# Loading q and k onto both row halves instead of copying between them, in an attention, expert and FFN kernel on one core

## The chip, the cores and the metric

The kernel runs on one core of a Trainium2 chip. A core has five engines with an instruction queue each: PE (TensorE, the matrix engine), DVE (VectorE), ACT (ScalarE), POOL (GpSimd) and SP (SyncE), which here only issues DMAs. The metric is the device time of one execution in microseconds (us), the median of several runs.

## What is computed

The reference chains three parts in float32, for batch B = 4 and 448 positions:

```python
# 1. causal attention, 12 heads of 64
scores = scale * q @ k^T ; scores = where(triu, -1e9, scores)
attn = exp(scores - max) ; attn = attn / (attn.sum + 1e-9)
x = (attn @ v)                       # -> (4, 448, 768)
# 2. four experts of width 64, each a causal attention on x; two of four chosen per position
q, k, v = x @ wq[e], x @ wk[e], x @ wv[e]
ye = softmax_causal(scale * q @ k^T) @ v @ wo[e]
out += gate_weight[e] * ye           # weights: softmax over the two largest of x @ w_gate
# 3. FFN with a convolution over positions
h = relu(out @ w_in)                 # 768 -> 1024
gate = sigmoid(conv3(h, conv_w))
result = (h * gate) @ w_out          # 1024 -> 768
```

## The kernel before

**Number format.** Where plain float32 would be slow, a value x is split into a high part (the copy rounded to the type fp32r) and a low part (x minus the high part), and a product is done as matmuls on the parts. For the scores of a head, which contract over 64 numbers only, the parts are stacked on the 128 rows: one half of the rows holds one part of q, the other half the other, and two matmuls per block (`for k in (2, 1)`, L580) run on all 128 rows.

**Heads and pairs.** Heads are handled in pairs (a "job"). There are 24 attention pairs A (6 per batch, `order` at L428 to L431) and 8 expert pairs M. Pair tensors in HBM have head 0 on rows 0 to 63 and head 1 on rows 64 to 127, q and k side by side.

**Preparing a pair** (`prep`, L515). An attention pair is loaded once as `nat`, 128 rows x 2 x 448 (L522). `hi` (L528) copies q and k to the high parts in `sk[0]`, `lo` (L532) subtracts for the low parts, in one instruction on POOL (L324). The parts now lie on the head's own half of the rows. `stack` (L457) moves them with five DMAs from SBUF to SBUF: three for head 1 (`go_b`, L467), then two for head 0 (`go_a`, L475). The first pair of all goes another way (`prep_twice`, L481): each head is loaded onto both halves by two DMAs, one on SP's queue and one on ACT's (L494), split at L497 and subtracted at L501 and L505, with no copies. Expert pairs come from a projection (`proj_qk`, L866) and use `stack` too.

**A head** (`head`, L559). Its 448 queries are four blocks of 112. For block i = 3, 2, 1, 0: two score matmuls (L581) of width 112 (i + 1) into a PSUM bank; DVE adds the causal mask, takes the row maximum and copies the scores out (`rowmax`, L594), which frees the bank; ACT takes the exponential with row sums (`soft`, L603). Then sums and reciprocals (L611, L614), normalisation (`norm`, L317 on POOL or L315 on ACT), transposes on PE (L634) into a bank and their copy to SBUF (`evac`, L315 or L321), and the products with v of both heads (L695, full float32, head h on output rows 64 h to 64 h + 63).

**Around it.** While the attention of batch 0 runs, `fold_all` (L756) multiplies the expert output weights into w_in: twelve pieces are loaded, converted from float64 bit by bit (`from_f64`, L372: four DVE and one ACT instruction), split and multiplied (L804). The projections of x (L880, L926) need its memory, so they start when it ends. The FFN (L1096 to L1160) starts when the projections are over and w_out is converted in the same way.

**What sets the order.** The kernel is a list of tasks with an engine (or several allowed ones, `ON`), an estimated cost, a priority, and ring buffers or PSUM banks taken and freed. `Program.run` (L129) simulates the engines with these costs when the kernel is built: whenever an engine is free it takes the ready task of lowest priority number whose buffers are free, and emits its instructions. On the chip each engine then runs its instructions in that fixed order. Priorities are 8 per job (`slot`) plus the numbers of `PR`; a task allowed on several engines carries an extra number (`PR["other"]`) on all but the first. A load counts 3200 ns to landing. A task with POOL among its engines, or marked `port`, holds a lock that keeps such tasks on DVE and POOL apart in the simulation. Where PE would be idle over 700 ns, `warm` (L1231) emits dummy matmuls on the identity (L1237) into an idle bank.

**Rings and banks.** `RINGS` gives the number of buffers (P = 3 for a head's scores, nat = 1, skA = 2 for the stacked parts of attention pairs), `BANKS` the PSUM banks per use: scores s = (0, 1), transposes t = (2, 3), products with v = (4, 5).

Of the kernel before, what the change touches and what calls it, by code (L numbers as in the profile page):

```python
# [16 lines left out]
AX = mybir.AxisListType  # L17

# [210 lines left out]
def attn_moe_ffn_kernel(  # L229
# [34 lines left out]
    BANKS = dict(s=(0, 1), t=(2, 3), v=(4, 5), m=(6, 7), h=(6, 7, 0, 2), o=(5, 3, 1))  # L264
    RINGS = dict(
        P=3, PT=4, osb=4, nat=1, skA=2, vn=3, vw=2, skM=1, vm=1, wg=2,
# [4 lines left out]
        load=(-823.5, 6881.0, -9741.0, -3861.0), prep=(-3868.5, 1311.5, -4485.0, 2630.5), wproj=-5653.5,  # L271
        fold0=2436.0, fold=6416.0, qk0=(-13000.5, -741.5, -2927.0, 9516.0), v=(1625.5, 634.5, 907.0, 9618.5),
        qk1=(9913.0, 10105.0, 5929.0, 31345.5), evac=-5114.5, conv=-6013.5,
        wo=(-7231.0, 5032.5, 7570.5, 14511.5, 8967.5, -5685.5), ffn0=564.5,
        ffn=(10002.0, -5113.5, 5693.5, -1579.0), out=(-702.0, 5485.0, -763.5, 1469.5),
        score=(8996.0, -638.0, 1743.0, -7812.5), rmax=(-1352.5, 6783.0, 22485.0, -7290.0),
        exp=(6192.0, 5875.5, 2412.5, 7853.5), norm=(4557.0, 1209.5, -5988.0, 7065.0),
        tr=(9656.0, -270.0, -15605.5, -1081.5), ev=(1749.0, 6735.5, -9228.0, 7657.5),
        pv=(-1538.5, 604.0, -2977.5, -6617.5), add=(-15863.0, 9244.5, -2422.5, -15681.0),
        slot=(-12628.0, 989.5, -130.0, -4172.5, 1485.5, 2137.0, -3585.0, -3863.5, -3413.5, -2921.5, -3458.0, -2327.0, -2434.0, -7790.5, -2832.0, 758.0, -1208.5, -1106.0, 8414.5, 976.0, 2099.0, 259.5, 4120.0, -1073.0, 3327.5, 6014.5, 6970.5, 8079.5, 6526.0, 4369.0, 3369.0, 3946.5),  # L280
        other=(8535.5, 4618.5, -2299.5, 867.0, 2856.0, 749.0, -4170.5), rows=(5476.0, 3097.0),
# [167 lines left out]
    def alloc_sk(j):  # L449
        n = f"{j.kind}{j.b}_{j.p}"  # L450
        pool = pools["head" if j.kind == "A" else "m"]
        j.sk = [
            pool.tile([P, 4 - h, S], F32R, tag=f"sk{h}", name=f"sk{h}_{n}", bufs=RINGS["sk" + j.kind])
            for h in range(2)
        ]
# [25 lines left out]
    def prep_twice(j):  # L481

        ready = {}
        for h in (1, 0):
            st = {}
            o = 1 - h

            def load(h=h, st=st):
                if h == 1:
                    alloc_sk(j)  # L490
                t = pools["a"].tile([P, TRI], F32, tag="PT", name=f"nat{h}", bufs=RINGS["PT"])
                st["nat"] = t[:, : 2 * S].rearrange("p (a n) -> p a n", a=2)
                for half in range(2):
                    (nc.scalar if half else nc.sync).dma_start(st["nat"][half * D : (half + 1) * D], qk[j.b, j.p, h * D : (h + 1) * D])  # L494

            def hi(h=h, st=st, o=o):
                nc.scalar.activation(j.sk[h][:, o : o + 3 : 2, :], st["nat"], AF.Copy)  # L497

            def lo_k(h=h, st=st, o=o):
                t = j.sk[h]  # L500
                nc.vector.tensor_tensor(t[:, o + 1, :], st["nat"][:, 1], f(t[:, o + 2, :]), ALU.subtract)  # L501

            def lo_q(h=h, st=st, o=o):
                q = j.sk[h][D:P, o, :]
                nc.vector.tensor_tensor(q, st["nat"][D:P, 0], f(q), ALU.subtract)  # L505

            pr = j.slot - 20 + o
            nb = Buf("PT")
            t = add("SP", pr, 1500, load, take=[j.skb, nb] if h == 1 else [nb], lag=3200)
            t = add("ACT", pr, act_sb(2 * S), hi, [t])  # L510
            tk = add("DVE", pr, dve(S), lo_k, [t], port=True)
            ready[h] = add("DVE", pr, dve(S), lo_q, [tk], free=[nb], port=True)
        return ready

    def prep(j):  # L515
        n = f"{j.b}_{j.p}"
        nat = Buf("nat")
        j.skb, j.vb = Buf("skA"), Buf("vn")

        def load():  # L520
            j.nat = pools["head"].tile([P, 2, S], F32, tag="nat", name=f"nat_{n}", bufs=1)
            nc.sync.dma_start(j.nat, qk[j.b, j.p])  # L522
# [5 lines left out]
        def hi(e):  # L528
            alloc_sk(j)
            copy(e, j.sk[0][:, 1:4:2, :], j.nat)  # L530

        def lo(e):  # L532
            t = j.sk[0]
            two(e, t[:, 0:3:2, :], j.nat, f(t[:, 1:4:2, :]), ALU.subtract)

        if j is order[0]:
            j.ready = prep_twice(j)
        else:
            t = add("SP", j.slot + PR["load"][j.phase], 1300, load, take=[nat], lag=3200)
            eng = either("q_hi", j.phase, of_one(2 * S))  # L540
            th = add(eng, j.slot + PR["prep"][j.phase], 0, hi, [t], take=[j.skb], free=[nat])
            eng = either("ql", j.phase, of_two(2 * S))
            tl = add(eng, j.slot + PR["prep"][j.phase], 0, lo, [th], free=[nat])
            stack(j, j.slot + PR["prep"][j.phase], [th, tl])
        j.vready = [add("SP", j.slot + PR["load"][j.phase] + 2, 700, load_v, take=[j.vb], lag=3200)]
# [3 lines left out]
    def attend(j):  # L549
# [4 lines left out]
        j.PT, j.evs = {}, []  # L554
        for h in (1, 0):
            head(j, h, moe)
        products_v(j, moe)

    def head(j, h, moe):  # L559
        n = f"{j.kind}{j.b}_{j.p}_{h}"  # L560
        prio = j.slot + 4 * (1 - h)
        st = {}
        Pb = Buf("P")
# [5 lines left out]
        def score(i):  # L569
            def go():  # L570
                if i == NQ - 1:
                    st["P"] = pools["a"].tile([P, TRI], F32, tag="P", name=f"P_{n}", bufs=RINGS["P"])[:CP]
                    st["sm"] = sums[n_head[0] % len(sums)]
                    n_head[0] += 1
                    for key in ("nm", "r"):
                        st[key] = pools["a"].tile([CP, NQ], F32, tag=key, name=f"{key}_{n}", bufs=RINGS["P"])
                w = CP * (i + 1)
                st["s", i] = sp = ps(st["sb", i])
                t = j.sk[h]
                for k in (2, 1):  # L580
                    nc.tensor.matmul(  # L581
                        sp[:CP, :w],
                        t[:, 1 - h, i * CP : (i + 1) * CP],
                        t[:, 1 - h + k, :w],
                        start=(k == 2),
                        stop=(k == 1),
                    )
# [714 lines left out]
```

## Time and profile before

| | us |
|---|---|
| median of 3 runs (lowest to highest) | 556.37 (553.23 to 557.66) |
| the profiled execution, its time | 555.16 |
| its span, first to last instruction | 553.4 |
| PE busy in the span | 517.9 |
| DVE busy, ACT busy, POOL busy | 348.1, 348.2, 226.5 |

The profile records one execution. A row of `xN` merges N instructions; "L581" is line 581 of the kernel. "PEq", "SPq" are sequencers. Matmuls are pipelined, so their durations overlap, and PE can be "busy" with dummy matmuls. What stands after an arrow is what ended an idle time.

### The profile page before, as it was taken

Reading aid. Unit: us, or ns where it says so; the run is one execution under the profiler, and the core shown is the slowest. Engines: PE = TensorE matmul, PEld = TensorE weight load, DVE = VectorE, ACT = ScalarE, POOL = GpSimd, SP = SyncE. Lnnn points to the kernel's source line nnn. Section 1 sums busy time; section 2 is a strip of 40 time slices with the busy share of each in tenths; the row PEclk is TensorE's granted clock in tenths of the full one; section 3 lists DMA queues with packets and bytes.
Section 4 is the critical chain, followed back from the end, with each engine's and each line's share of the span. In section 5 each row is a group of like instructions: output and inputs, shape, how many; then the busy total and the mean of one; then the engine's idle time right before and its main releaser. Section 6 shows DMA issues by size and latency. Waiting matters only on the chain.

```text
span 553.4 us, 10183 instructions
## 1 busy us (share of the span) xinstructions
PE 517.9 (94%) x3306; PEld 439.3 (79%) x3306; DVE 348.1 (63%) x1081; ACT 348.2 (63%) x931; POOL 226.5 (41%) x375
## 2 busy tenths in 40 slices
PE   6977979999998989999989999997999999999997
PEld 6766757878786777888768887876789999899996
DVE  3778988685475574766652856578999914955000
ACT  3869989786575675578764865559868504844111
POOL 1555566645564465575544643362543110000000
PEclk8889999999999998999999999998999999999999
DMA  8889986887648376749396134352130210010111
GB/s 251 239 213 234 232 234 162 245 207 173 157 101 184 93 168 166 174 111 221 85 199 158 25 76 124 106 132 58 38 116 34 71 51 33 18 42 26 50 51 66
DMA packets 28230, 70.91 MB, mean 128 GB/s; under 512 B 4433, under 2 KB 12241, under 8 KB 28177
## 3 DMA queue, kind: packets, MB, share of 16 engines
q1 hardware_dynamic: 28016, 69.80, 49.1%
q8 instruction: 26, 0.43, 0.3%
q10 hardware_dynamic: 160, 0.46, 0.3%
q14 instruction: 28, 0.22, 0.1%
HBM read 32.74 MB, written 5.51 MB: 69 GB/s over the span
## 4 chain that ended last, share of the span: by engine, by line
PE 61%; DMA 14%; DVE 11%; POOL 5%; ACT 4%; issue 3%; SPq 3%; POOLq 0%; ACTq 0%; DVEq 0%
PE bank L1160 18%; PE bank L880 10%; PE bank L581 10%; PE bank L634 7%; DMA sk_A<-sk_A 7%; PE bank L695 7%; DMA nat<-in_qk_dram 4%; PE bank L1096 4%; PE bank L926 4%; DVE bank L1117 3%; POOL sk_A L324 3%; SPq L467 2%; DMA woraw<-in_w_out_dram 2%; DVE g L1134 1%; DVE P_A L594 1%
## 5 line engine op out<-in xcount | busy, mean ns | idle before, releaser
L1160 PE MATMUL bank<-g,wout 128*128 128x448 f32 x576 | 119.4, 366 | 0.0
L603 ACT ACTIVATE P_A<-P_A,nm_A 112x448 f32<-112x448 f32 x192 | 99.6, 521 | 26.7 <-DVE nm_A L594 24.9
L1160 PEld LDWEIGHTS bank<-g,wout 128*128 128x128 f32 x576 | 108.1, 188 | 8.8
L317 POOL TENSOR_SCALAR P_A<-P_A,r_A 112x336 f32<-112x336 f32 (+3 forms) x169 | 83.6, 513 | 67.0 <-DVE r_A L614 43.9
L594 DVE CUSTOM_DVE_ANT_0 P_A<-bank,mask 112x448 f32<-112x448 f32 x192 | 80.8, 442 | 40.2 <-PE bank L581 33.3
L581 PE MATMUL bank<-sk_A 128*112 128x112 f32 (+3 forms) x384 | 81.9, 324 | 17.7 <-DMA sk_A<-sk_A 10.4
L581 PEld LDWEIGHTS bank<-sk_A 128*112 128x112 f32 x384 | 58.1, 182 | 31.6 <-DVE nm_A L594 10.5
L880 PE MATMUL bank<-xT,wqk 128*128 128x448 f32 x288 | 75.0, 381 | 0.1
L324 POOL TENSOR_TENSOR sk_A<-nat,sk_A 128x896 fp32r<-128x896 f32 x23 | 48.6, 2112 | 44.4 <-ACT sk_A L315 35.8
L634 PE MATMUL bank<-ident,P_A 112*112 112x112 f32 x480 | 64.8, 265 | 2.1 <-ACT PT_A L315 1.6
L634 PEld LDWEIGHTS bank<-ident,P_A 112*112 112x112 f32 x480 | 51.2, 135 | 7.2 <-POOL P_A L317 1.1
L1117 DVE SCALAR_TENSOR_TENSOR bank<-h,cw,bank 128x448 f32<-128x448 f32 x64 | 42.2, 682 | 17.0 <-ACT bank L1115 16.8
L880 PEld LDWEIGHTS bank<-xT,wqk 128*128 128x128 f32 x288 | 49.9, 191 | 3.0 <-DVE wqk L856 0.5
L695 PE MATMUL bank<-PT_A,v 112*64 112x448 f32 (+3 forms) x384 | 51.3, 408 | 0.0
L315 ACT ACTIVATE osb<-bank 128x448 f32<-128x448 f32 x18 | 9.8, 543 | 61.1 <-PE bank L1160 61.1
L1096 PE MATMUL bank<-ocs,wp 128*128 128x448 f32 x192 | 43.9, 376 | 2.8 <-DVE g L1134 2.0
L321 DVE TENSOR_SCALAR PT_A<-bank 112x448 f32<-112x448 f32 (+1 forms) x71 | 38.8, 556 | 11.4 <-PE bank L634 9.9
L695 PEld LDWEIGHTS bank<-PT_A,v 112*64 112x64 f32 x384 | 25.8, 137 | 24.6 <-issue 13.9
L926 PE MATMUL bank<-wvg,xT 128*112 128x260 f32 x288 | 45.2, 293 | 0.1
L315 ACT ACTIVATE PT_A<-bank 112x336 f32<-112x336 f32 (+1 forms) x73 | 32.8, 464 | 17.9 <-PE bank L634 13.9
L317 POOL TENSOR_SCALAR P_M<-P_M,r_M,g_w 112x448 f32<-112x448 f32 (+3 forms) x58 | 33.2, 584 | 23.0 <-DVE r_M L614 15.0
L1096 PEld LDWEIGHTS bank<-ocs,wp 128*128 128x128 f32 x192 | 36.1, 192 | 7.7 <-DVE g L1134 3.3
(103 smaller groups left out, 811.6 us busy)
## 6 DMA issues: line engine op xcount, KB each, us to landing
nat<-in_qk_dram SPq DMA_DIRECT2D x23, 448.0 KB, 5.1
sk_A<-sk_A SPq DMA_DIRECT2D x46, 224.0 KB, 4.2
sk_A<-sk_A SPq DMA_DIRECT2D x23, 336.0 KB, 3.5
wraw<-in_w_in_dram SPq DMA_DIRECT2D x12, 512.0 KB, 6.0
woraw<-in_w_out_dram SPq DMA_DIRECT2D x12, 512.0 KB, 4.0
v<-in_v_dram SPq DMA_DIRECT2D x24, 224.0 KB, 5.2
out_dram<-osb SPq DMA_DIRECT2D x24, 224.0 KB, 1.9
sk_A<-sk_A SPq DMA_DIRECT2D x46, 112.0 KB, 4.3
```

The source lines that it names most:

```text
L317: nc.gpsimd.tensor_scalar(dst, src, scale, 1.0 if scale2 is None else scale2, ALU.mult, ALU.mult)
L324: (nc.gpsimd if e == "POOL" else nc.vector).tensor_tensor(dst, a, b, op)
L581: nc.tensor.matmul(sp[:CP, :w], t[:, 1 - h, i * CP : (i + 1) * CP], t[:, 1 - h + k, :w], start=(k == 2), stop=(k == 1),)
L594: nc.vector.tensor_tensor_reduce(rows(i), st["s", i][:CP, :w], mask[:, S - w :], -SCALE, 3.0e38, ALU.add, ALU.min, st["nm"][:, i : i + 1],)
L603: nc.scalar.activation(rows(i), rows(i), AF.Exp, bias=st["nm"][:, i : i + 1], scale=-1.0, accum_out=st["sm"][:, i, 0:1],)
L634: nc.tensor.transpose(pt[:CP, o : o + CP], rows(i)[:, kt * CP : (kt + 1) * CP], ident[:CP, :CP])
L695: nc.tensor.matmul(st["ov"][h * D : (h + 1) * D, kt * CP : S], j.v[:, kt, h, :], j.PT[h][:, col_base[kt] : col_base[kt] + S - kt * CP], st ...
L880: nc.tensor.matmul(st["ps"][:, :S], proj["wqk"][:, a, cc, w, p * P : (p + 1) * P], xT[b, cc][:, b2, :], start=(cc == 0 and (a, b2) == PASS ...
L926: nc.tensor.matmul(st[i][:CP, :VW], xT[b, cc][:, a, i * CP : (i + 1) * CP], proj["wvg"][:, b2, cc, :], start=(cc == 0 and (a, b2) == PASSE ...
L1096: nc.tensor.matmul(st["ps", c][:, :S], wp[:, a, ec, c * P : (c + 1) * P], st["oc", ec][:, b2], start=(ec == 0 and (a, b2) == PASSES[0]), s ...
L1117: nc.vector.scalar_tensor_tensor(y, h, w, y, ALU.mult, ALU.add)
L1160: nc.tensor.matmul(st["ps"][:, :S], ffn["wout", n][:, a, c], gs[c][:, b2], start=(c == 0 and (a, b2) == PASSES[0]), stop=(c == NFC - 1 and ...
```

## The change

1. The first two attention pairs of batch 0 (`j.plain`) are loaded once and used as they are: scores in plain float32, q and k of a head on its own 64 rows, one matmul per block and head, both heads' matmuls one after the other in one task (`pair_scores`). Pair 0 is loaded in two halves, on ACT's and SP's queues; pair 1 in one DMA.
2. All other attention pairs are loaded like the first pair before: each head onto both halves of the rows by two DMAs of 64 rows (both on SP), then one split and two subtractions per head. The split may go to the engines of `q_hi` as before (ACT alone after batch 0), the subtractions to POOL or DVE (before: POOL). `stack` stays for expert pairs. `sk[0]` of attention pairs has three rows instead of four.
3. Blocks 1 and 0 of a head's scores share one bank, written by one task; row maxima, exponentials and the rest stay as they are. Score banks become (0, 1, 4), transpose banks (2, 3, 5).
4. P = 4 instead of 3 (with a fourth `sums` tile), nat = 2 instead of 1.
5. All numbers of `PR` are new, and the planner's cost term PVX is 10 instead of 55.

```diff
-    BANKS = dict(s=(0, 1), t=(2, 3), v=(4, 5), m=(6, 7), h=(6, 7, 0, 2), o=(5, 3, 1))
+    BANKS = dict(s=(0, 1, 4), t=(2, 3, 5), v=(4, 5), m=(6, 7), h=(6, 7, 0, 2), o=(5, 3, 1))
     RINGS = dict(
-        P=3, PT=4, osb=4, nat=1, skA=2, vn=3, vw=2, skM=1, vm=1, wg=2,
+        P=4, PT=4, osb=4, nat=2, skA=2, vn=3, vw=2, skM=1, vm=1, wg=2,
...
-        ql=('P', 'P', 'P', 'P'), norm=('PA', 'P', 'P', 'PD'), vm=('AD', 'A', 'A', 'A'), q_hi=('DAP', 'A', 'A', 'A'),
+        ql=('PD', 'PD', 'PD', 'P'), norm=('PA', 'P', 'P', 'PD'), vm=('AD', 'A', 'A', 'A'), q_hi=('DAP', 'A', 'A', 'A'),
...
-    PVX = 55
+    PVX = 10
...
+        j.plain = j.kind == "A" and j.b == 0 and j.p < 2
...
+            def go():
                 if h == 1:
                     alloc_sk(j)
...
+                st["nat"] = pools["head"].tile([P, 2, S], F32, tag="nat", name=f"nat_{n}_{h}", bufs=RINGS["nat"])
                 for half in range(2):
...
+                    nc.sync.dma_start(st["nat"][half * D : (half + 1) * D], qk[j.b, j.p, h * D : (h + 1) * D])
...
+        def hi(h, st):
+            return lambda e: copy(e, j.sk[h][:, 0:3:2, :], st["nat"])
+
+        def lo_k(h, st):
+            return lambda e: two(e, j.sk[h][:, 1, :], st["nat"][:, 1], f(j.sk[h][:, 2, :]), ALU.subtract)
+
+        def lo_q(h, st):
+            return lambda e: two(e, j.sk[h][D:P, 0, :], st["nat"][D:P, 0], f(j.sk[h][D:P, 0, :]), ALU.subtract)
+
+        def load_plain():
+            alloc_sk(j)
+            j.qk = f(j.sk[0][:, 0:2, :])
+            if j is order[0]:
+                for h in range(2):
+                    (nc.sync if h else nc.scalar).dma_start(j.qk[h * D : (h + 1) * D], qk[j.b, j.p, h * D : (h + 1) * D])
+            else:
+                nc.sync.dma_start(j.qk, qk[j.b, j.p])
...
+        if j.plain:
+            t = add("SP", j.slot + PR["load"][j.phase], 1300, load_plain, take=[j.skb], lag=3200)
+            j.ready = [t, t]
         else:
...
+            for h in (1, 0):
+                st, nat = {}, Buf("nat")
+                pr = j.slot + PR["prep"][j.phase] + 1 - h
+                take = [j.skb, nat] if h else [nat]
+                t = tl = add("SP", j.slot + PR["load"][j.phase] + 1 - h, 1400, load(h, st), [tl], take=take, lag=3200)
+                t = add(either("q_hi", j.phase, of_one(2 * S)), pr, 0, hi(h, st), [t])
+                eng = either("ql", j.phase, of_two(S))
+                tk = add(eng, pr, 0, lo_k(h, st), [t], free=[nat])
+                j.ready[h] = add(eng, pr, 0, lo_q(h, st), [tk], free=[nat])
...
+    def pair_scores(j):
...
+                w = CP * (i + 1)
+                for h in (1, 0):
...
+                    r = slice(h * D, (h + 1) * D)
+                    nc.tensor.matmul(
+                        sp[:CP, :w], j.qk[r, 0, i * CP : (i + 1) * CP], j.qk[r, 1, :w], start=True, stop=True
+                    )
...
+                for m, o in ((i, 0),) if i > 1 else ((1, 0), (0, 2 * CP)):
+                    w = CP * (m + 1)
+                    st["s", m] = sp = ps(st["sb", i])[:, o : o + w]
```

## Rows read from the trace of the kernel before

**Rows 1.** Windows, five stages: busy us (instructions) per engine, granted clock, DMA share, GB/s.

```profile
0.00:20.00 20.00, 15.42 (x78) 13.96 (x79) 8.85 (x35) 10.80 (x26) 5.65 (x17) 0.83 0.84 249
20.00:97.00 77.00, 66.25 (x488) 53.28 (x486) 66.32 (x200) 65.79 (x182) 44.41 (x47) 0.98 0.86 217
97.00:365.00 268.00, 257.42 (x1832) 212.03 (x1831) 165.53 (x650) 176.78 (x535) 145.29 (x252) 0.99 0.59 143
365.00:420.00 55.00, 49.30 (x283) 41.53 (x283) 49.24 (x99) 42.30 (x91) 22.49 (x38) 0.97 0.33 91
420.00:553.40 133.40, 129.48 (x635) 118.45 (x633) 58.13 (x100) 52.58 (x100) 8.64 (x24) 1.00 0.12 44
sum 553.40, PE 517.86 PEld 439.26 DVE 348.07 ACT 348.24 POOL 226.49; mean PE 103.57 PEld 87.85 DVE 69.61 ACT 69.65 POOL 45.30
```

**Rows 2.** The same windows, the dummy matmuls of L1237 alone: PE, weight loads.

```profile
0.00:20.00 20.00, 10.17 (x56) 9.88 (x56) 0.83 0.84 249
20.00:97.00 77.00, 3.03 (x20) 2.55 (x20) 0.98 0.86 217
97.00:365.00 268.00, 0.62 (x4) 0.53 (x4) 0.99 0.59 143
365.00:420.00 55.00, 9.77 (x74) 9.02 (x74) 0.97 0.33 91
```

**Rows 3.** PE's waits, 0 to 97 us: total us, times, longest.

```profile
PE bank L581 <- DMA sk_A<-sk_A: 6.6, 5, 2.5
PE bank L581 <- DVE nm_A L594: 3.3, 7, 1.1
```

**Rows 4.** PE's waits, 97 to 365 us.

```profile
PE bank L581 <- DMA sk_A<-sk_A: 3.8, 4, 2.1
PE bank L581 <- DVE nm_M L594: 3.3, 2, 2.7
```

**Rows 5.** Time line of the start: start us, us, engine, line, operation, idle before.

```profile
6.80 1.28 ACT L497 ACT_TABLE_LOAD   x1 [6.80 <-DMA nat<-in_qk_dram]
...
10.49 1.36 PE L581 MATMUL bank<-sk_A 128*112 128x448 f32 x4 [2.23 <-DVE sk_A L505]
...
23.34 0.95 PE L581 MATMUL bank<-sk_A 128*112 128x448 f32 x4
24.22 2.11 PE L695 MATMUL bank<-PT_A,v 112*64 112x448 f32 x16
...
36.74 0.63 PE L581 MATMUL bank<-sk_A 128*112 128x448 f32 x2 [2.46 <-DMA sk_A<-sk_A]
```

**Rows 6.** The page's DMA issues: count, KB each, median us to landing.

```profile
nat<-in_qk_dram SPq DMA_DIRECT2D x23, 448.0 KB, 5.1
sk_A<-sk_A SPq DMA_DIRECT2D x46, 224.0 KB, 4.2
sk_A<-sk_A SPq DMA_DIRECT2D x23, 336.0 KB, 3.5
...
sk_A<-sk_A SPq DMA_DIRECT2D x46, 112.0 KB, 4.3
```

**Rows 7.** Groups by line and form: busy us, mean ns, idle before.

```profile
L315 ACT ACTIVATE sk_A<-nat 128x896 fp32r<-128x896 f32 x21 | 19.9, 948 | 22.3 <-DMA nat<-in_qk_dram 14.5 <-PE bank L581 4.2 <-PE bank L634 2.5
...
L1078 POOL TENSOR_TENSOR ocs<-oc,ocs 128x448 fp32r<-128x448 f32 x8 | 9.1, 1147 | 0.2
...
L501 DVE TENSOR_TENSOR sk_A<-nat,sk_A 128x448 fp32r<-128x448 f32 x2 | 1.3, 626 | 8.1 <-ACT sk_A L497 8.1
```

**Rows 8.** ACT's waits, 97 to 365 us.

```profile
ACT sk_A L315 <- DMA nat<-in_qk_dram: 13.2, 7, 3.7
```

**Rows 9.** The instructions of L856 on DVE: ns min/median/max, first and last start.

```profile
L856 DVE TENSOR_TENSOR wqk<-praw,wqk x6: 674/680/1216, 95.6 to 112.9; 128x512 fp32r<-128x512 f32 x6
```

**Rows 10.** Time line of POOL and DVE around 110 us.

```profile
108.94 2.11 POOL L324 TENSOR_TENSOR sk_A<-nat,sk_A 128x896 fp32r<-128x896 f32 x1 [0.53 <-ACT sk_A L315]
...
110.38 1.22 DVE L856 TENSOR_TENSOR wqk<-praw,wqk 128x512 fp32r<-128x512 f32 x1
```

More of the change, by code (lines that the diff above doesn't have):

```diff
@@ L451, in alloc_sk @@
         pool = pools["head" if j.kind == "A" else "m"]
+        j.o = (0, 0) if j.kind == "A" else (1, 0)
         j.sk = [
-            pool.tile([P, 4 - h, S], F32R, tag=f"sk{h}", name=f"sk{h}_{n}", bufs=RINGS["sk" + j.kind])
+            pool.tile([P, 3 if j.kind == "A" else 4 - h, S], F32R, tag=f"sk{h}", name=f"sk{h}_{n}", bufs=RINGS["sk" + j.kind])
             for h in range(2)
@@ L479, in stack, with prep, load @@
         j.ready = [ta, tb]
[L481 to L488, printed above, removed]
+    def prep(j):
+        n = f"{j.b}_{j.p}"
+        j.skb, j.vb = Buf("skA"), Buf("vn")
+        def load(h, st):
+            def go():
                 if h == 1:
                     alloc_sk(j)
-                t = pools["a"].tile([P, TRI], F32, tag="PT", name=f"nat{h}", bufs=RINGS["PT"])
-                st["nat"] = t[:, : 2 * S].rearrange("p (a n) -> p a n", a=2)
+                st["nat"] = pools["head"].tile([P, 2, S], F32, tag="nat", name=f"nat_{n}_{h}", bufs=RINGS["nat"])
@@ L507, in prep_twice @@
[L507 to L522, printed above, removed]
+                    nc.sync.dma_start(st["nat"][half * D : (half + 1) * D], qk[j.b, j.p, h * D : (h + 1) * D])
@@ new lines, in load @@
+            return go
+        def hi(h, st):
[12 more added lines that the diff above has]
+                nc.sync.dma_start(j.qk, qk[j.b, j.p])
@@ L526, in load_v @@
             nc.sync.dma_start(j.v, v[j.b, j.p])
[L528 to L537, printed above, removed]
-        else:
[L539 to L544, printed above, removed]
+        if j.plain:
+            t = add("SP", j.slot + PR["load"][j.phase], 1300, load_plain, take=[j.skb], lag=3200)
+            j.ready = [t, t]
+        else:
+            j.ready = {}
+            tl = None
+            for h in (1, 0):
[7 more added lines that the diff above has]
+                j.ready[h] = add(eng, pr, 0, lo_q(h, st), [tk], free=[nat])
         j.vready = [add("SP", j.slot + PR["load"][j.phase] + 2, 700, load_v, take=[j.vb], lag=3200)]
@@ L554, in attend @@
         j.PT, j.evs = {}, []
+        j.st = {h: {} for h in (1, 0)}
+        if j.plain:
+            pair_scores(j)
         for h in (1, 0):
@@ L561, in head @@
         prio = j.slot + 4 * (1 - h)
-        st = {}
-        Pb = Buf("P")
+        st = j.st[h]
+        Pb = st["Pb"] if j.plain else Buf("P")
         ex, nm = {}, {}
@@ L571, in go @@
                 if i == NQ - 1:
[L572 to L587, printed above, removed]
+                    head_tiles(j, h)
+                for m, o in ((i, 0),) if i > 1 else ((1, 0), (0, 2 * CP)):
+                    w = CP * (m + 1)
+                    st["s", m] = sp = ps(st["sb", i])[:, o : o + w]
+                    t = j.sk[h]
+                    for k in (2, 1):
+                        nc.tensor.matmul(
+                            sp[:CP],
+                            t[:, j.o[h], m * CP : (m + 1) * CP],
+                            t[:, j.o[h] + k, :w],
+                            start=(k == 2),
+                            stop=(k == 1),
+                        )
             return go
@@ L651, in head @@
             w = CP * (i + 1)
-            sb = st["sb", i] = Buf("s")
-            t = add(
-                "PE", prio + PR["score"][j.phase], mm(w, 2), score(i), [j.ready[h]] + (first or late),
-                take=[sb] if first else [sb, Pb], free=[j.skb],
-            )
-            if not first:
-                first = j.taken = [t]
+            if j.plain:
+                t = j.scored[i]
+                sb = st["sb", i]
+            elif i:
+                sb = st["sb", i] = Buf("s")
+                t = add(
+                    "PE", prio + PR["score"][j.phase], mm(w, 2) + (mm(CP, 2) if i == 1 else 0), score(i), [j.ready[h]] + (first or late),
+                    take=[sb] if first else [sb, Pb], free=[j.skb],
+                )
+                if not first:
+                    first = j.taken = [t]
+                ts = t
+            else:
+                t = ts
             t = add("DVE", prio + PR["rmax"][j.phase], dve(w) + 8, rowmax(i), [t], free=[sb])
```

63 lines of the change are left out of this document (43 added, 20 removed).

## The prediction

> **What bounds the kernel now.** I read the table of stages first [rows 1]. PE is busy 517.86 of 553.40 us, so 35.54 us are idle. Part of the busy time does no work: the planner fills gaps with dummy matmuls (L1237), nearly all in three stages [rows 2]. Idle plus dummy time is the most that better feeding of PE can return in a stage:
>
> 0 to 20: 20.00 - 15.42 + 10.17 = 14.8 us. 20 to 97: 77.00 - 66.25 + 3.03 = 13.8 us. 97 to 365: 268.00 - 257.42 + 0.62 = 11.2 us. 365 to 420: 55.00 - 49.30 + 9.77 = 15.5 us. 420 to the end: 3.9 us.
>
> So there are two kinds of stage. Up to 97 us, where the attention of batch 0 runs beside the folding of the weights, no engine is full: from 20 to 97 DVE works 66.32 and ACT 65.79 of 77 us (86% and 85%), and the DMA share is 0.86. That is a pipeline that starts late and is then near several limits at once. From 97 to 365 PE is 96% busy and is the bound; only its gaps can go. From 365 on the FFN runs, which the edit touches by its new order numbers alone.
>
> Next I read who ends PE's waits [rows 3, 4]. Up to 97 us the copies between row halves end 6.6 us of them and DVE's row maxima 3.3 us. From 97 to 365 the copies of the attention pairs end 3.8 us and the row maxima 3.3 us. The time line of the start shows the lag behind these sums [rows 5]: the first pair's scores start at 10.49 us, the second's at 23.34, the third's at 36.74, the last straight after a wait for a copy.
>
> **The first two pairs in plain rows.** Pair 0 loses the load of its data onto both halves (four loads of 224 KB become two), two ACT splits and four DVE subtractions; pair 1 loses one ACT split, a POOL subtraction of 2.1 us and five copies. ACT today waits until 6.80 us for data, then comes its table load of 1.28 us, then the splits [rows 5]. In plain rows PE can start when the data lands. I take the 6.8 us of the row, though half the bytes should land sooner: 10.49 - 6.8 = 3.7 us earlier. If the table load then stands ahead of the first exponential, that gives back up to 1.3 us; ends -3.7 and -2.4, I take -3.
>
> PE itself pays in full float32: eight matmuls on 64 rows per pair instead of sixteen on 128. The trace has none on 64 rows. The nearest are the products with v, also float32 and with the same columns (448, 336, 224 and 112 for each of two heads), the two heads on different halves of the output: 16 of them in 2.11 us [rows 5]. If the two row halves overlap as these output halves do, a pair's scores cost 2.1 us; if not, twice that, 4.2. Today the four wide score matmuls of a head take 0.95 us [rows 5]; the four narrow ones have 43% of their columns, so a pair is 2 x 0.95 x 1.43 = 2.7 us. The change is between -0.6 and +1.5 us per pair; PE has 14.8 us to spare in this stage, so I cost it at nothing. Without that cover it is at most 3 us.
>
> Pair 1 no longer waits for load, split, subtraction and two rounds of copies. Its scores can follow pair 0's by about 3 us instead of 12.9. Its softmax then fills DVE and ACT time that is empty now: before 20 us DVE works 8.85 and ACT 10.80 us [rows 1].
>
> **Both halves loaded, no copies (22 pairs).** Removed per pair: one load of 448 KB and five copies, 2 x 224 + 336 + 2 x 112 = 1008 KB [rows 6]; added: four loads of 224 KB. So 1456 KB become 896. Six such pairs (numbers 2 to 7) load before 97 us: 3.4 MB less of the 21.7 MB moved there (249 GB/s for 20 us and 217 for 77), so the DMA share falls from 0.86 to about 0.7 at an equal rate. On SP seven issues per pair (with v) become five, and the waits of the copies for POOL go. What remains there is the wait of a load for its buffer, now also for the pair's tile, with v and weight loads queued behind it.
>
> The ready time of a pair shortens by two rounds of copies, 3.5 to 4.3 us to landing each [rows 6]. In return there is more to compute. ACT: two splits of 0.95 us instead of one. The subtractions: one POOL instruction of 2.11 us becomes four, of 1.15 us each on POOL (4.6 us) or 0.63 us on DVE (2.5 us) [rows 7, 10]. The planner prefers POOL and gives to DVE when DVE has nothing else; I take half each, +0.2 us on POOL and +1.25 us on DVE per pair. The ends are all on POOL (+2.5 us there per pair) and all on DVE (+2.5 us there, -2.1 on POOL). From 97 to 365 this lies beside PE: ACT works 177, DVE 166 and POOL 145 of 268 us, so 16 pairs x 0.95 = 15 us more on ACT is hidden by 91 idle us; on the path it would be 15 us. Before 97 us it is not wholly hidden: ACT gets 6 x 0.95 less the three splits saved, +2.9 us, DVE 6 x 1.25 less 2.5 saved, +5 us, against 10.7 and 11.2 idle us from 20 to 97. I count half of DVE's, 2.5 us.
>
> ACT also waits in order for loads, 13.2 us in 7 waits from 97 to 365 [rows 8], with exponentials and evacuations behind. There will be twice as many such instructions, on loads that meet 38% less traffic of q and k; I take no change.
>
> **Three banks, two blocks in one.** A head takes three score buffers instead of four, from three banks instead of two, and a fourth P buffer lets a further head start. This acts on PE's waits for row maxima, 3.3 us before 97 and 3.3 after [rows 3, 4]. It adds no instruction; the row maximum of the second last block waits for the two small matmuls of the last. Bounds 0 and 6.6 us; I take 1 us of the first, where copies would soon end the wait instead, and half of the second, 1.7.
>
> **New order numbers.** They move every engine's order. I cannot derive a sign; I take 0 within 4 us either way for the stages from 365 on (19.4 us of idle plus dummy time).
>
> **Sum.** Up to 97 us: start -3, copies ahead of PE -6.6, banks -1, DVE +2.5: -8. From 97 to 365: copies -3.8, banks -1.7, of which 2 us return as waits for the last subtraction: -3.5. The granted clock is 0.98 from 20 to 97 and 0.99 from 97 to 365 [rows 1], 0.02 x 77 + 0.01 x 268 = 4.2 us; with fewer gaps I take back 1.5. Total -13. The span goes from 553.4 to 540.4 us. The profiled execution took 555.16 us, 1.8 us around its span, so 542.2 us; it lay 1.2 us under the median of the runs (556.37), so I predict **543 us**, 13.4 us or 2.4% below.
>
> **Rivals.**
>
> *Hidden anyway, about 553 us.* From 20 to 97 us DVE and ACT are already 86% and 85% busy and get more work. If they, not the copies, set the pace of 12 to 13 us per pair, the 6.6 us only change their name. Then the 3 us of the start remain and the rest is given back as waits on subtractions: 556.4 - 3 = 553. For it: those two shares. Against: DVE's idle time in that stage is 10.7 us, and PE's waits there name copies. It includes the case that the change does not do what it says, because a subtraction queued behind normalisations on POOL is ready as late as the copy was.
>
> *Slower, about 564 us.* DVE and POOL get in each other's way. One case shows it [rows 9, 10]: the subtraction at L856 has a median of 680 ns, but the one that began at 110.38 us, while a POOL subtraction of 2.11 us was running since 108.94, took 1216 ns: 0.54 us lost. If all 88 new subtractions lose that, 47 us of stalls arise on the two engines, with row maxima behind them on DVE and normalisations on POOL. If 45% of it reaches PE the price is 21 us, 543 + 21 = 564. It decides the sign once more than 28% (13.4 us) gets through. Against it: POOL is 54% busy from 97 to 365, so many meet no POOL instruction, and DVE has 102 idle us there.
> The Trainium skill states the rule in "SBUF — State Buffer", section "SBUF: two separate sides": a DVE instruction with two SBUF inputs and a GpSimd instruction that reads SBUF exclude each other for the whole instruction. The case above agrees.
>
> *Better, about 530 us.* The start runs a full 10 us ahead, DVE and ACT fill up to 97 us, and the gaps from 97 to 365 go entirely: -15 and -11 us. For it: pairs 1 and 2 can be ready 10 us or more earlier. Against: the stages from 365 on do not shrink, and the added ACT and DVE work is real.
>
> **How the numbers follow.** Forecast 0.53, better 0.20, hidden 0.16, slower 0.11. A measurement of this kernel tells about 1% from no change, here 5.6 us. Faster by over 1%: all of "better" and all of the forecast, whose own range is 536 to 549: 0.73. Same: 0.16. Slower: 0.11. The range for 8 in 10 reaches into both neighbours: 530 to 557 us.
>
> **What would show it.** Right: first scores near 7 us, the second pair's near 10; no copies of attention data left; PE's waits for them gone with little in their place; the first projection matmul well before 97 us; the DMA share near 0.7 up to there. Wrong: PE waiting for subtractions on POOL or DVE by the 10.4 us that the copies cost (6.6 + 3.8); subtractions on DVE near 1.2 us; ACT waiting over 25 us for loads; dummy matmuls after 365 us growing past 9.8 us.

## Result and profile after

The changed kernel takes 538.69 us (535.41 to 540.93) against 556.49 us for the kernel before: ratio 0.972, 95% interval 0.968 to 0.976. (The quotient of the two medians is 0.968, at the edge of that interval; the comparisons below go by such ratios.) The forecast was 543 us, in a range of 530 to 557. The profiled execution took 538.64 us, its span 536.8.

The stages in the same windows as [rows 1] (busy us per engine, granted clock, DMA share, GB/s):

```profile
0.00:20.00 20.00, 15.74 (x85) 13.16 (x86) 8.50 (x40) 9.71 (x30) 5.44 (x15) 0.91 0.95 234
20.00:97.00 77.00, 73.79 (x578) 60.55 (x578) 71.91 (x223) 72.43 (x201) 61.90 (x78) 1.00 0.63 177
97.00:365.00 268.00, 262.15 (x1899) 219.00 (x1896) 188.02 (x677) 196.17 (x571) 156.30 (x258) 1.00 0.44 111
...
sum 536.80, PE 517.81 PEld 442.35 DVE 364.10 ACT 361.10 POOL 249.84; mean PE 103.56 PEld 88.47 DVE 72.82 ACT 72.22 POOL 49.97
```

From 20 to 97 us DVE and ACT are now busy 93% and 94% of the time (86% and 85% before) and the DMA share is 0.63 instead of 0.86. PE's idle time over the span fell from 35.5 to 19.0 us, but its busy time is the same, 517.8 us, and it holds more dummy matmuls, 34.3 us (L1280) against 23.6. So PE's useful busy time, without the dummies, fell by 10.8 us, though the work is the same but for two pairs.

To see where the end moved, I cut the windows at the first FFN matmul. Its start, before and after, from the time lines:

```profile
367.76 1.47 PE L1096 MATMUL bank<-ocs,wp 128*128 128x448 f32 x6
```

```profile
351.69 1.48 PE L1139 MATMUL bank<-ocs,wp 128*128 128x448 f32 x6
```

It comes 16.1 us earlier, and the end of the span 16.6 us. What follows takes as long as before, 185.1 us against 185.6. The two stages ahead of it, before:

```profile
0.00:97.00 97.00, 81.66 (x563) 67.25 (x563) 75.17 (x235) 76.59 (x208) 50.06 (x63) 0.95 0.86 223
97.00:367.80 270.80, 260.21 (x1853) 213.55 (x1852) 168.33 (x655) 177.90 (x537) 147.64 (x257) 0.99 0.59 143
```

and after, with the dummies of L1280 alone in the same windows below:

```profile
0.00:97.00 97.00, 89.53 (x660) 73.71 (x662) 80.41 (x263) 82.14 (x230) 67.34 (x93) 0.98 0.70 189
97.00:351.70 254.70, 251.73 (x1837) 209.77 (x1833) 178.97 (x650) 186.09 (x546) 153.67 (x255) 1.00 0.44 110
```

```profile
0.00:97.00 97.00, 19.73 (x132) 18.09 (x132) 0.98 0.70 189
97.00:351.70 254.70, 4.66 (x30) 3.90 (x30) 1.00 0.44 110
```

Up to the FFN, idle plus dummy time went from 25.9 + 13.8 = 39.7 us to 10.4 + 24.4 = 34.8 us. That is 4.9 us: 1.3 us up to 97 us (28.5 to 27.2) and 3.6 us from there to the FFN (11.2 to 7.6). The other 11.2 us are useful busy time, 328.0 against 316.9 us.

About half of that goes with the clock. At 0.95 and 0.99 the old stages lacked 0.05 x 97 + 0.01 x 271 = 7.6 us of full speed, the new ones 0.02 x 97 = 1.9, so 5.7 us; summed in windows of 2 us, with the dummies left out, it is 7.3 against 0.9 us. The old kernel's granted clock is at or near half speed (0.50, 1.2 GHz) from about 10 to 18 us and in three later spells, here with PE first; in each of them PE is busy all the time:

```profile
38.00:42.00 4.00, 4.00 (x24) 4.00 (x24) 3.15 (x14) 3.42 (x12) 3.53 (x3) 0.57 0.58 144
178.00:182.00 4.00, 4.00 (x19) 3.73 (x18) 2.40 (x12) 2.27 (x8) 2.23 (x4) 0.57 0.84 179
208.00:212.00 4.00, 4.00 (x19) 3.41 (x21) 1.80 (x9) 2.34 (x8) 1.92 (x4) 0.59 0.98 222
```

They lack 5.1 us of full speed. Each comes soon after one of PE's three longest waits of that stretch, the one that ends at 36.74 us [rows 5] and these two:

```profile
176.37 0.40 PE L581 MATMUL bank<-sk_M 128*112 128x112 f32 x2 [2.69 <-DVE nm_M L594]
...
207.92 0.94 PE L581 MATMUL bank<-sk_A 128*112 128x448 f32 x4 [2.08 <-DMA sk_A<-sk_A]
```

Two of the three are waits for copies. In the changed kernel PE never waits over 1.6 us at once between 20 us and the FFN, and up to there the clock is below 0.9 only from 14 to 20 us. Not every such wait has a spell behind it (in e9 below, one of 2.1 us for a copy has none), and no run changes the clock alone, so that the waits bring the spells is likely but not shown.

The other half goes with longer runs of the same operation. The matmuls of the two projections come in some 70 and 45 stretches before and in some 40 and 16 after, and their groups take less busy time (PE, busy us and mean ns), first before, then after; what such a run is worth by itself is not tested:

```profile
L880 PE MATMUL bank<-xT,wqk 128*128 128x448 f32 x288 | 75.0, 381 | 0.1
...
L926 PE MATMUL bank<-wvg,xT 128*112 128x260 f32 x288 | 45.2, 293 | 0.1
```

```profile
L923 PE MATMUL bank<-xT,wqk 128*128 128x448 f32 x288 | 67.2, 373 | 0.0
...
L969 PE MATMUL bank<-wvg,xT 128*112 128x260 f32 x288 | 38.2, 286 | 0.5 <-DVE sk_M L939 0.5
```

PE's waits up to 97 us, and from 97 to 365, answering [rows 3, 4]:

```profile
PE bank L574 <- DMA sk_A<-in_qk_dram: 2.2, 1, 2.2
...
PE bank L617 <- DVE sk_A L325: 0.9, 1, 0.9
PE bank L617 <- POOL sk_A L325: 0.9, 3, 0.4
...
PE bank L574 <- DVE nm_A L630: 0.3, 1, 0.3
```

```profile
PE bank L617 <- DMA sk_M<-sk_M: 2.7, 1, 2.7
...
PE bank L617 <- DVE sk_A L325: 0.3, 1, 0.3
PE bank L617 <- DVE nm_M L630: 0.2, 1, 0.2
```

The 10.4 us for copies are gone, and the subtractions that replace them (L325) cost PE 2.1 us. The waits for row maxima fell from 6.6 us to 0.5. The 2.7 us for copies of an expert pair end at 361.75 us, behind the first FFN matmul.

The start, answering [rows 5]:

```profile
9.03 1.01 PE L574 MATMUL bank<-sk_A 64*112 64x448 f32 x4 [2.15 <-DMA sk_A<-in_qk_dram]
...
15.19 2.30 PE L617 MATMUL bank<-sk_A 128*112 128x448 f32 x8 [0.44 <-POOL sk_A L325]
...
30.69 1.01 PE L574 MATMUL bank<-sk_A 64*112 64x448 f32 x4
```

Pair 0 starts 1.5 us earlier than before. The second to start is a split pair (L617, 15.19 us against 23.34 for the second pair before); the second plain pair follows only at 30.69. The new order put it there.

### The profile page after: what moved, and what is told of

The parts are those of the page before. It is cut to its first block, busy times and chain, and to the rows that moved or that the text cites. A ratio compares the mean times of both kernels' runs of the same rounds, so it can differ in the third digit from the quotient of the medians.

```text
span 536.8 us, 10287 instructions
## 1 busy us (share of the span) xinstructions
PE 517.8 (96%) x3392; PEld 442.4 (82%) x3392; DVE 364.1 (68%) x1102; ACT 361.1 (67%) x962; POOL 249.8 (47%) x404
## 4 chain that ended last, share of the span: by engine, by line
PE 70%; ACT 10%; DVE 8%; DMA 4%; POOL 4%; issue 2%; SPq 1%; DVEq 0%; ACTq 0%; POOLq 0%
PE bank L1203 20%; PE bank L738 9%; PE bank L617 9%; PE bank L670 8%; PE bank L923 8%; PE bank L969 7%; PE bank L1139 6%; ACT P_A L639 3%; PE bank L1280 2%; DMA nat<-in_qk_dram 2%; PE bank L847 2%; ACT sk_A L316 2%; POOL P_A L318 1%; DMA woraw<-in_w_out_dram 1%; POOL sk_A L325 1%
## 5 line engine op out<-in xcount | busy, mean ns | idle before, releaser
L318 POOL TENSOR_SCALAR P_A<-P_A,r_A 112x448 f32<-112x448 f32 (+3 forms) x175 | 97.5, 575 | 41.3 <-DVE r_A L650 20.2
L639 ACT ACTIVATE P_A<-P_A,nm_A 112x448 f32<-112x448 f32 (+1 forms) x192 | 99.6, 523 | 10.9 <-DVE nm_A L630 9.4
L630 DVE CUSTOM_DVE_ANT_0 P_A<-bank,mask 112x448 f32<-112x448 f32 (+1 forms) x192 | 77.8, 442 | 13.6 <-PE bank L574 9.2
L923 PE MATMUL bank<-xT,wqk 128*128 128x448 f32 x288 | 67.2, 373 | 0.0
L617 PE MATMUL bank<-sk_A 128*112 128x448 f32 (+3 forms) x352 | 64.3, 314 | 2.5 <-DVE sk_A L325 1.3
L325 POOL TENSOR_TENSOR sk_A<-nat,sk_A 64x448 fp32r<-64x448 f32 (+1 forms) x46 | 55.8, 1212 | 19.3 <-DVE sk_A L322 11.2
L617 PEld LDWEIGHTS bank<-sk_A 128*112 128x112 f32 x352 | 49.1, 178 | 9.2 <-POOL sk_A L325 1.8
L318 POOL TENSOR_SCALAR P_M<-P_M,r_M,g_w 112x336 f32<-112x336 f32 (+3 forms) x58 | 34.9, 615 | 37.8 <-DVE r_M L650 16.4
L639 ACT ACTIVATE P_M<-P_M,nm_M 112x448 f32<-112x448 f32 (+1 forms) x64 | 33.1, 519 | 12.3 <-DVE nm_M L630 12.1
L316 ACT ACTIVATE sk_A<-nat 128x896 fp32r<-128x896 f32 x39 | 36.7, 945 | 5.2 <-DMA nat<-in_qk_dram 5.0
```

The source lines that it names most:

```text
L316: nc.scalar.activation(dst, src, AF.Copy, scale=scale)
L318: nc.gpsimd.tensor_scalar(dst, src, scale, 1.0 if scale2 is None else scale2, ALU.mult, ALU.mult)
L325: (nc.gpsimd if e == "POOL" else nc.vector).tensor_tensor(dst, a, b, op)
L617: nc.tensor.matmul(sp[:CP], t[:, j.o[h], m * CP : (m + 1) * CP], t[:, j.o[h] + k, :w], start=(k == 2), stop=(k == 1),)
L630: nc.vector.tensor_tensor_reduce(rows(i), st["s", i][:CP, :w], mask[:, S - w :], -SCALE, 3.0e38, ALU.add, ALU.min, st["nm"][:, i : i + 1],)
L639: nc.scalar.activation(rows(i), rows(i), AF.Exp, bias=st["nm"][:, i : i + 1], scale=-1.0, accum_out=st["sm"][:, i, 0:1],)
```

## Experiments

All ratios are to the kernel before, timed on the same chip in the same session; two experiments are compared by their ratios. "Fitted" means that the numbers of PR were searched anew for that structure: a random search changes one to three of them at a time and keeps what shortens the planner's own estimate.

**e1: one cost term of the planner.** `PVX = 10` back to 55 in the changed kernel.

```diff
-    PVX = 10
+    PVX = 55
```

> The changed kernel (538.7 us) with the planner's cost term PVX at 55 as before instead of 10: the same instructions in a slightly other order. It measures what an order that fits a little less well costs by itself. If orders matter little: 535 to 543 us. If the new order numbers carry the gain and are finely fitted to their costs: 545 us or more.

Measured 549.41 us, ratio 0.987 (0.980 to 0.994). Nothing but the order differs (and the dummies that go with it), and by the ratios 1.5% is lost, over half of the gain. Another order of the same instructions moves the time as much as a whole part of the change.

**e2: all parts, old order.** The changed kernel with PR and PVX of before.

```diff
-    PR = dict(load=(-2419.0, 19933.0, ...
-    PVX = 10
+    PR = dict(load=(-823.5, 6881.0, ...
+    PVX = 55
```

> The changed kernel with all order numbers and PVX of before: every structural part of the change, none of the new order. Theory 'structure' (no copies and the earlier start give most of it): 541 to 548 us. Rival 'order' (the new numbers give it): 553 us or more.

Measured 558.29 us, ratio 1.007 (1.004 to 1.011): 0.7% slower than before. The parts alone, under the order written for the old kernel, bring nothing. No attention copies are left to wait for and the granted clock is 1.00 in every stage, but up to 365 us PE is idle for 14.0 us and on dummies for 34.2, together 48.2 us against 39.7 before [rows 1, 2]. The gaps are now in the plan, where the dummies fill them.

**e3: new order, no part.** The kernel before with PR and PVX of the change.

```diff
-    PR = dict(load=(-823.5, 6881.0, ...
-    PVX = 55
+    PR = dict(load=(-2419.0, 19933.0, ...
+    PVX = 10
```

> The kernel before with the new order numbers and PVX = 10, nothing else. Theory 'structure': no gain, 554 to 565 us, since PE still waits for copies. Rival 'order': 548 us or less.

Measured 599.89 us, ratio 1.079 (1.073 to 1.084), far above both ranges. PE's longest wait in total is for row maxima, which free the score banks:

```profile
PE bank L581 <- DVE nm_A L594: 12.8, 23, 3.2
```

"Order" (the new numbers give the gain by themselves) falls by e3, and "structure" as e2 states it falls by e2: order numbers belong to one structure. To compare parts, each variant needs an order of its own.

**e4: halves alone, old order.** The kernel before with the new `prep` for all pairs but the first, nat = 2 and ql on POOL or DVE.

```diff
-        P=3, PT=4, osb=4, nat=1, skA=2, vn=3, vw=2, skM=1, vm=1, wg=2,
+        P=3, PT=4, osb=4, nat=2, skA=2, vn=3, vw=2, skM=1, vm=1, wg=2,
...
-        ql=('P', 'P', 'P', 'P'), norm=...
+        ql=('PD', 'PD', 'PD', 'P'), norm=...
...
-            stack(j, j.slot + PR["prep"][j.phase], [th, tl])
+            for h in (1, 0):
...
+                j.ready[h] = add(eng, pr, 0, lo_q(h, st), [tk], free=[nat])
```

> The kernel before with one part of the change: q and k loaded onto both halves for all attention pairs (nat = 2, subtractions on POOL or DVE), no copies for them; old banks, old order numbers, no plain pairs. Theory 'copies': they are the largest part, 543 to 549 us. Rival 'hidden anyway': 553 us or more, the added splits and subtractions on ACT, DVE and POOL take back what the copies cost.

Measured 568.08 us, ratio 1.022 (1.017 to 1.027). By itself it could mean "hidden anyway"; after e2 and e3 it can as well be the order, which was written for another structure; e11 separates the two.

**e5: copies back, fitted.** The changed kernel with the preparation of before for all but the plain pairs.

```diff
-            for h in (1, 0):
-                st, nat = {}, Buf("nat")
...
+            t = add("SP", j.slot + PR["load"][j.phase], 1300, load1, take=[nat], lag=3200)
...
+            stack(j, j.slot + PR["prep"][j.phase], [th, tl])
```

> The changed kernel with the preparation of before put back for all but the two plain pairs (one load, one split, one subtraction, five copies) and everything else kept, its order numbers searched anew for this structure with the planner's own estimate, which comes out 1% shorter than for the changed kernel. Theory 'slip': copies land later than the planner counts, so the chip falls behind the plan: 548 to 558 us. Rival 'fit': only the fit of the order to the structure matters: 531 to 541 us.

Measured 549.56 us, ratio 0.995 (0.991 to 0.999), as "slip" expects, though the planner expects less time than for the changed kernel. PE's waits name the copies:

```profile
PE bank L640 <- DMA sk_A<-sk_A: 9.0, 7, 3.2
PE bank L693 <- DVE xT L786: 4.8, 1, 4.8
```

**e6: the kernel before, fitted in the same way.** Only PR (and PVX = 10) differ from the kernel before.

```diff
-        load=(-823.5, 6881.0, -9741.0, -3861.0), ...
+        load=(-985.0, 80089.0, 46435.0, -47006.5), ...
-    PVX = 55
+    PVX = 10
```

> The kernel before (all its parts, PVX = 10) with order numbers searched anew in the same way; the planner expects 1% less than for the changed kernel. Theory 'slip': 546 to 558 us, no better than before. Rival 'fit': 530 to 541 us, the changed kernel's gain without any of its parts.

Measured 561.32 us, ratio 1.016 (1.008 to 1.024). "Fit" falls: an order that the planner likes better than the changed kernel's is 4.5% slower than it on the chip when the structure is the old one. The time is also above the 558 us of "slip", and the new order is 1.6% slower than the one that this structure had: the planner's estimate does not rank orders of one structure that closely. PE waits 6.9 us for copies of attention pairs and 4.1 for those of expert pairs:

```profile
PE bank L595 <- DMA sk_A<-sk_A: 6.9, 6, 1.9
...
PE bank L595 <- DMA sk_M<-sk_M: 4.1, 3, 2.1
```

**e7: no plain pairs, fitted.**

```diff
-        j.plain = j.kind == "A" and j.b == 0 and j.p < 2
+        j.plain = False
```

> The changed kernel without plain pairs (pairs 0 and 1 split and loaded on both halves like the others), order searched anew; the planner expects 0.5% more. If plain rows give the 3 us of the start that the prediction counts: 541 to 547 us. If they give nothing: 536 to 541 us.

Measured 541.87 us, ratio 0.978 (0.972 to 0.985). The time lies in the range of "they give the 3 us", and the ratio is 0.6% (3.5 us) above the changed kernel's. But the two intervals overlap, so the plain pairs' share cannot be told from nothing.

**e8: old banks, fitted.**

```diff
-    BANKS = dict(s=(0, 1, 4), t=(2, 3, 5), v=(4, 5), m=(6, 7), h=(6, 7, 0, 2), o=(5, 3, 1))
+    BANKS = dict(s=(0, 1), t=(2, 3), v=(4, 5), m=(6, 7), h=(6, 7, 0, 2), o=(5, 3, 1))
```

> The changed kernel with the PSUM banks of before, s = (0, 1) and t = (2, 3), the last two blocks still in one bank, order searched anew; the planner expects 0.3% more. If the third bank gives the 2.7 us counted: 540 to 545 us. If it gives nothing: 536 to 540 us.

Measured 547.99 us, ratio 0.991 (0.986 to 0.996), more than either theory gave. Not by PE's waits for row maxima, 1.7 us up to 97 us in this run; the larger ones there are for subtractions on DVE and for the plain data:

```profile
PE bank L631 <- DVE sk_A L339: 4.4, 4, 2.1
PE bank L588 <- DMA sk_A<-in_qk_dram: 3.7, 2, 2.4
```

and the granted clock is 0.96 from 0 to 97 us, with a spell near half speed from 20 to 28 us around the waits for the plain data. PE's work comes later; the first FFN matmul starts at 360.2 us. Which of these the banks cause and which this order, the run does not tell.

**e9: copies back, planned with later landings, fitted.** As e5, with longer delays in the planner.

```diff
-        tb = add("SP", prio, 1900, go_b, need, lag=3300)
-        ta = add("SP", prio, 1400, go_a, need + [tb], lag=3300)
+        tb = add("SP", prio, 1900, go_b, need, lag=4800)
+        ta = add("SP", prio, 1400, go_a, need + [tb], lag=4800)
...
-            t = add("SP", j.slot + PR["load"][j.phase], 1300, load1, take=[nat], lag=3200)
+            t = add("SP", j.slot + PR["load"][j.phase], 1300, load1, take=[nat], lag=4400)
```

> As e5 (copies back in the changed kernel), but the planner now counts 1.5 us more to the landing of each round of copies and 1.2 us more for the loads, and the order is searched anew under these delays; it expects 0.2% more than for the changed kernel. Theory 'slip' (the copies cost mainly because the order was written for landings that come late): 538 to 545 us, waits of PE for copies under 4 us. Rival 'copies cost by themselves' (their time cannot be hidden by any order): 547 us or more, waits as in e5.

Measured 548.54 us, ratio 0.987 (0.982 to 0.992). PE's waits for these copies halve, 9.0 to 4.1 us:

```profile
PE bank L640 <- DMA sk_A<-sk_A: 4.1, 3, 2.1
PE bank L640 <- DMA sk_M<-sk_M: 3.2, 3, 1.9
```

Against e5 that is 0.8%, with intervals that overlap a little, and 1.5% remain to the changed kernel. The time is that of the rival, the waits nearly those of "slip". The DMA share stays high, 0.94 up to 97 us. But the first FFN matmul starts at 353.8 us, only 2.1 us after the changed kernel's, and the part behind it is longer, 190.3 us against 185.1:

```profile
0.00:97.00 97.00, 87.27 (x647) 70.54 (x648) 76.82 (x255) 78.69 (x227) 51.56 (x73) 1.00 0.94 243
97.00:353.80 256.80, 249.96 (x1819) 208.56 (x1817) 155.78 (x612) 173.15 (x528) 129.87 (x235) 1.00 0.55 133
353.80:544.10 190.30, 180.61 (x946) 163.06 (x944) 112.66 (x204) 95.88 (x190) 31.21 (x60) 1.00 0.18 61
```

PE has the same number of expert attention and FFN matmuls left there as in the changed kernel, but 15.2 us of dummies instead of 10.0, and DVE has 8 us more to do. So in this execution, the shortest of the four, most of what remains is the end of this order and not a wait for attention copies.

**e10: the changed kernel, another fitted order.** Only PR and PVX = 55 differ; searched from the numbers of before.

```diff
-        load=(-2419.0, 19933.0, -1009.0, -12634.5), ...
+        load=(-2062.0, 9389.5, -7161.0, -39769.0), ...
-    PVX = 10
+    PVX = 55
```

> A control: the changed kernel's structure with another order, searched from the order numbers of before with PVX = 55; the planner expects 0.5% more than for the changed kernel. It shows how far two searched orders of the same structure lie apart on the chip. If a searched order is worth little noise: 538 to 545 us, and e5, e6 stand apart from it. If the changed kernel's order was singled out: 548 us or more, and then e5 to e8 prove nothing about their parts.

Measured 542.0 us, ratio 0.974 (0.969 to 0.980). Two orders found apart from each other, for the same structure, agree within 0.3%. Other such pairs lie further apart: e5 and e9, whose planned delays differ, 0.8%, the kernel before and e6 1.6%. So a single difference of 1 to 2% between two variants need not be the worth of a part.

**e11: halves alone on the kernel before, fitted.** e4 with an order of its own; the diff is to e4.

```diff
-        load=(-823.5, 6881.0, -9741.0, -3861.0), ...
+        load=(-5425.0, 13790.5, -20718.5, 18620.5), ...
```

> As e4 (the kernel before with loads onto both halves, old banks, P = 3, first pair as before), with its order searched anew; the planner still expects 1.8% more than for the changed kernel. If halves with a fitted order carry the gain: 541 to 548 us. If they need the third bank and the fourth P buffer: 550 us or more.

Measured 549.58 us, ratio 0.989 (0.984 to 0.993). Halves alone gain 1.1%, 3.3% more than with the old order (e4); the time lies between the two expectations. Against the change this kernel lacks the third banks, the shared bank, the fourth P buffer and the plain pairs. PE's longest total wait is for row maxima, and so for banks, again:

```profile
PE bank L607 <- DVE nm_A L620: 5.7, 13, 1.6
```

**e12: three P buffers, fitted.**

```diff
-        P=4, PT=4, osb=4, nat=2, skA=2, vn=3, vw=2, skM=1, vm=1, wg=2,
+        P=3, PT=4, osb=4, nat=2, skA=2, vn=3, vw=2, skM=1, vm=1, wg=2,
```

> The changed kernel with three P buffers instead of four, order searched anew; the planner expects 0.6% less. If the fourth buffer gives slack against delays that the planner does not see: 541 to 548 us. If it gives nothing: 534 to 540 us.

Measured 534.58 us, ratio 0.963 (0.958 to 0.968): faster than both kernels, by 0.9% than the changed one. The fourth buffer gives nothing that can be seen; whether three are better or this order is, one order of e12 does not tell. Its windows, cut at the first FFN matmul:

```profile
0.00:97.00 97.00, 89.19 (x651) 70.98 (x652) 85.89 (x269) 83.14 (x231) 62.27 (x85) 1.00 0.68 187
97.00:348.80 251.80, 249.42 (x1831) 210.28 (x1829) 176.46 (x643) 188.20 (x549) 151.40 (x257) 1.00 0.44 111
348.80:532.30 183.50, 175.49 (x894) 158.71 (x892) 105.30 (x193) 93.64 (x188) 29.09 (x56) 0.99 0.17 58
```

DVE does 85.9 us by 97 us, against 80.4 in the changed kernel: the start is packed more closely, and the clock is 1.00 from 0 to 97.

**The fitted orders together.** With the halves and all banks, four of them measure 2.2 to 3.7% below the kernel before (the change, e7, e10, e12). With only one of the two parts, four measure 0.5 to 1.3% below it (e5, e8, e9, e11). With neither, e6 is 1.6% above it. The ratios of the groups do not overlap, though the intervals of e7 and e9 do. This is the best evidence here that both parts are needed, with an order of their own.

## Why the prediction was right, and where not

The sign and the size held: 2.4% forecast, 2.8% measured. The term for the copies held in kind. PE's waits for them went (10.4 us to none), 2.1 us came back as waits for subtractions (2 counted), and the end moved by as much as the FFN's start. That the removal counts, and not only a fitted order, is supported by e5 and e9: with the copies put back, neither order gained more than 1.3%, and without them and with all banks no fitted order gained less than 2.2%. That the added work does not take it back follows from the same runs.

The near hit of the sum is in part luck. I counted 8 us less idle plus dummy time up to 97 us, 3.5 from there on and 1.5 for the clock. It fell by 1.3 and 3.6 us. The 11.2 us of useful busy time that made up for the missing 6.7 were in my sum only as the 1.5 of the clock.

**New order numbers at 0 within 4 us: the step that failed.** With the old numbers the whole gain is gone (e2, 558 us), with one cost term changed over half of it (e1). I treated order as a small unknown beside the parts; it is the condition under which they work. The forecast could come out because the change brings an order made for its structure.

**Banks at 1 + 1.7 us: mis-sized, it seems.** Taken away, with the order fitted, they cost 1.7 to 1.9% (e8 against e10 and the change), some 10 us, though with one order of e8 alone. Halves without them give 1.1% (e11), they without halves 0.5 to 1.3% (e5, e9), the whole 2.6 to 2.8%. That the parts are worth more together than one by one is not shown: 1.1 and 1.3 add up to 2.4, and the intervals reach 0.4 to 0.5 either way. How the banks act is not settled: in e8 PE waits little for row maxima.

**Clock and PE's own time: mis-sized.** I counted idle plus dummy time as all that can return and 1.5 us for the clock. Idle plus dummy time up to the FFN returned 4.9 us; 11.2 us came from useful busy time, of which the granted clock accounts for about 6. A busy PE is not a PE at its pace. The executions of the kernel before, all one list of instructions, show what the clock is worth: 548.5 us at a granted clock of 0.997, 558.9 us at 0.971, about 3 us for each hundredth over 33 executions. At 0.994 one took 549.0 us and one of the changed kernel, in another session, 538.6: at a like clock some 10 of the 18 us between the medians are left.

**The start: wrong in detail.** The first scores come at 9.03 us, not 6.8, because the half loaded through SP is issued at 2.58 us, behind four weight loads there (from 0.73 us on), and the second plain pair starts at 30.69, not 10. The table load costs nothing: it runs on ACT at 1.31 us, before any data is there. The first projection matmul was to come well before 97 us; it came at 97.1 before and comes at 126 now, since the order does more attention first. So that sign of being right failed, though the FFN starts earlier. Plain rows cannot be told from nothing (e7). Their scores cost 3.0 us for the second pair, between the 2.1 and 4.2 given.

**Work per pair: held.** The subtractions split 46 on POOL and 42 on DVE, half each as taken:

```profile
L325 POOL TENSOR_TENSOR sk_A<-nat,sk_A x46: 1130/1150/1596, 12.8 to 298.8; 64x448 fp32r<-64x448 f32 x28, 128x448 fp32r<-128x448 f32 x18
...
L325 DVE TENSOR_TENSOR sk_A<-nat,sk_A x42: 612/626/1315, 22.3 to 303.8; 128x448 fp32r<-128x448 f32 x26, 64x448 fp32r<-64x448 f32 x16
```

**Rival "hidden anyway": fell** for the fitted kernels; it is what e2 and e4 look like from outside. DVE and ACT did become nearly full in the start (93% and 94%), but at a higher pace. **Rival "slower" by stalls between DVE and POOL: its mechanism is there, its size is not.** The longest subtraction on DVE took 1315 ns; it began at 87.58 us, while a POOL subtraction of 1.27 us (L838) was running since 87.14. The exclusion described in the Trainium skill ("SBUF — State Buffer", section "SBUF: two separate sides") would have it wait in this way, and the trace agrees. The medians, 626 and 1150 ns, are at the means of [rows 7], 626 and 1147, and the groups' busy times exceed 42 x 0.626 and 46 x 1.150 us by 4.1 us on DVE (30.4 in all) and 2.8 us on POOL (55.7): 7 us, not 47. **Rival "better":** the changed kernel is 9 us short of its 530. The first scores come 1.5 us earlier and not 10; the second pair's come 8 us earlier.

**ACT's waits for loads at no change: wrong in my favour.** From 97 to 365 us they fell from 13.2 [rows 8] to 4.8 us, though ACT has 39 such splits instead of 21 in the span.

**Why copies hurt more than planned.** The planner counts a load of before as landed 1.3 + 3.2 = 4.5 us after its start; the median was 5.1 [rows 6]. For the first round of copies it counts 1.9 + 3.3 = 5.2 us; the third copy starts about 1.5 us after the first and lands 4.2 later. For the second round it counts 1.4 + 3.3 = 4.7 us; the second copy starts about 1.1 us after the first and lands 4.2 later. The new loads are planned at 1.4 + 3.2 = 4.6 us; the second of two issued 0.6 us apart lands at 0.6 + 3.9 us:

```profile
nat<-in_qk_dram SPq DMA_DIRECT2D x88, 224.0 KB, 3.9
```

So by the medians the old structure runs about half a microsecond behind its plan at each of three steps of a pair, and the new one runs on it. e9, which plans for the delay, halves the waits and recovers 0.8% of the 2.3% between e5 and the change. That this slip is part of the cause is supported by the waits, but not cleanly by the time. What the remaining 1.5% is stays open; in the traces 5.2 of the 7.3 us between e9 and the change lie behind the first FFN matmul, in the end of that order. A second way in which copies cost more than their waits is the clock, which is near half speed after two of the waits for them.

## What to carry to other kernels

Where a program's order is written ahead from estimated delays, a change of structure is judged only with an order of its own: the same parts measured +0.7% with the old order and -2.6 to -2.8% with either of two fitted ones. Steps that land later than planned can cost more than their waits show, because every engine's fixed order behind them runs late; planning such a step nearer to its measured time halved the waits here, and removing it did more. A planner's estimate does not stand in for the chip: for e6 it lay 1% below that for the changed kernel, and e6 was 4.5% slower. And a buffer added is not a gain by itself: the version with one fewer was the fastest.

## What the runs showed of the hardware that I had not expected

A float32 matmul leaves two records in the trace: 192 products with v are x384, while 384 score matmuls of the split kind are x384. The rows that I read as 16 products are eight; their price, 2.11 us, stays the same.

Two float32 matmuls on the two row halves take about as long as two on the two output halves: the widest two of a plain pair 1.01 us, the widest two products 0.97 us. A whole plain pair still took 3.0 us at a granted clock of 1.00, and not the 2.11 of eight products in a row. Its four blocks were issued apart, each after other work; the 16 matmuls of the split pair that comes second in the kernel before, also issued apart, took 2.96 us.

The granted clock of PE was 0.98 instead of 0.95 from 0 to 97 us, and 1.00 instead of 0.99 from there to the FFN, while PE's idle time up to the FFN fell from 25.9 to 10.4 us and its dummy time rose from 13.8 to 24.4. Fewer and shorter gaps came with a faster clock. A faster clock alone does not make the kernel fast: e2 had 1.00 in every stage and took 558 us.
